# Order of a visit, z of early pairs, and where second-stage weights are decoded, in a fused linear-attention and feed-forward kernel

## The chip, the cores and the metric

The kernel runs on one core of a Trainium2 chip. The core has five instruction queues that run side by side and wait for each other through semaphores: TensorE (PE in the profile; PEld is its weight loading), VectorE (DVE), ScalarE (ACT), GpSimd (POOL) and SyncE (SP), which here only issues DMAs. PE writes its results to PSUM, from where DVE and ACT take them. The metric is the time of one execution on the device, in microseconds; lower is better.

## The reference

There are 8 batches of 8 heads, 576 tokens and head size 64. Then the heads are joined to 4608 tokens of 512 features, which go through a feed-forward network (FFN) of 2048 hidden features.

```python
def phi(x):
    proj = np.einsum('bhsd,df->bhsf', x, w_phi)            # 64 -> 128 features
    proj = proj - np.max(np.abs(proj), axis=-1, keepdims=True)
    return np.concatenate([np.exp(proj), np.exp(-proj)], axis=-1)
q_p, k_p = phi(q), phi(k)
kv  = np.einsum('bhsf,bhsd->bhfd', k_p, v)
z   = np.sum(k_p, axis=2)
num = np.einsum('bhsf,bhfd->bhsd', q_p, kv)
den = np.einsum('bhsf,bhf->bhs', q_p, z)[..., None] + 1e-06
x   = joined heads of num / den                            # 4608 x 512
h = x @ w_in                                               # 512 -> 2048
g = np.maximum(h, 0.0) + alpha * np.minimum(h, 0.0)
out = g @ w_out                                            # 2048 -> 512
```

The FFN's weights are double precision. The kernel gets them as pairs of 32-bit words, decodes them, and splits each into a high and a low part. Activations are split in the same way, so each FFN product is three matmuls: high by high, low by high, high by low (L494 to L496 and L500 to L502).

## The kernel before

**Attention by pairs.** Two heads make a pair; 32 pairs are numbered in the order in which they run (four pairs to a batch). The work on one pair is spread over several *visits*: in visit j, PE works on the projections of pairs j and j+1, on kv and z of pair j-1, and on the numerators and denominators of pair j-2. The names in the profile are:

- `raw`: k and q as loaded; `pj`, `pl`: their projections in PSUM (L297). DVE takes the largest magnitude of each row (`m`, L300) and subtracts it (`t`, L301).
- `xk`, `k` (in the program `k4`): exponentials of k, four full tiles of 128 tokens and one of 64, on ACT (L314, L309).
- `kv`: one PSUM tile with k's features by v (L338) and, in its third part, z (L355), by a product with ones. `y` and `z` on DVE (L323 to L331) add the k tiles before that product. For pairs below ZP = 9, called early here, only `y` is made, which adds tiles in twos, and PE adds up the rest; for the others DVE adds up all five tiles.
- `ks`, `kt`, `sf`: the copy of `kv` on ACT (L365), its transpose on PE (L370), and the copy of that (L374). `qt`, `qf`: the transposed t of q (L381, L384) and its exponentials (L392, L394).
- `n`: numerators (L403), two halves, copied by ACT to `s` (L414). `d`: denominators (L421), copied to `ds` (L431). A small DMA lays them out over partitions, DVE inverts them (L440, L441), a DMA writes them to HBM (`rec_d`), another spreads them over the rows (`rr`, L449), POOL multiplies (L454), and a DMA stores the tokens (`x_d`, L457).

`pl` of one head, `kt`, `qt`, the two halves of `n` and `d` all take turns in two PSUM buffers (`ps_m`). A projection takes turns in three others.

**The FFN in two stages.** Hidden blocks of 128 are numbered 0 to 15. The first stage (blocks 0 to 4) runs over nine chunks of 512 tokens while attention is still running: a visit holds some 30 FFN matmuls. Its partial results go to HBM (`part_d`). The second stage (blocks 5 to 15) goes over all chunks again, adds the partial results and stores. For each block, ACT takes two halves of the activation from PSUM (`r`, `g`, L228, L229), DVE joins them (`g`, L233), ACT casts the high part (`gh`, L119), DVE subtracts to get the low part (`gl`, L123). The tokens are split likewise, into `xh` (DVE, L120) and `xl` (POOL, L123).

**Decoding.** A weight block is decoded in four pieces of 256 columns: load (SP, L152), scale (ACT, L163), split (four DVE instructions, L171 to L174), add (POOL, L179), high (ACT, L119), low (POOL, L123), store. Blocks 0 to 4 come in the early visits, two pieces to a visit. Blocks 5 to 9 come from visit 12.5 on, 0.95 visits apart, and are stored to HBM (`w_d`); at the turn to the second stage, when attention's memory is free, they are loaded by DMAs that POOL issues. Blocks 10 to 12 are decoded in place from time 37.8 on. Blocks 13 to 15 are decoded after the first stage has closed, between the products of the second.

**What sets the order.** All the work up to that close is a list of small functions, each with a time in units of a visit. The list is sorted by time, and PE, SP, DVE and ACT execute in just that order; POOL's order is left to a scheduler. The function `places` (L57) holds the times of attention's steps after the pair's number: `ka` is kv, `kz` z, `p` the projections, `n` and `d` the numerators and denominators, `s` and `ds` their copies, `ko` the copy of kv, `ks` DVE's sums of k. `FG` (L93) holds the times of the join, the cast and `gl` after a block's last matmul; `WT` (L95) those of a decode's stages.

## Time and profile before

| | us |
|---|---|
| median of 3 runs (lowest to highest) | 1194.63 (1193.9 to 1195.11) |
| the profiled execution, in all | 1196.74 |
| its span from the first to the last instruction | 1195.0 |
| mean granted TensorE clock | 0.989 |
| chain that ended last: share of PE, of DVE | 53%, 4% |
| HBM traffic | 103 GB/s over the span |

An instruction of the profile is given by its engine, source line and operands, out<-in, with the buffers' numbers left out. A row of a wait says who waited for whom. A row of a timeline begins with the start in us from the beginning of the span and the duration; what stands in brackets is the idle time of that engine before it and what ended that. A PE matmul's end is modelled. Attention runs until about 560 us; the first stage's last chunks close at about 660 us; what follows is the second stage alone.

### The profile page before, as it was taken

How to read it: one execution, taken by the hardware profiler on the slowest of the kernel's cores; microseconds unless marked ns; L12 is line 12 of the kernel's file. 1: busy time of each engine (PE TensorE's matmuls, PEld its weight loads, DVE VectorE, ACT ScalarE, POOL GpSimd, SP SyncE). 2: the span in 40 equal slices, each digit the busy share in tenths (PEclk: the TensorE clock that was granted, in tenths of full speed). 3: DMA queues.
4: the chain of work that ended last, by engine and by line, in shares of the span. 5: the costliest groups of instructions: out<-in, count | busy, mean ns of one | idle time of the engine just before them, and what ended most of it. 6: DMA issues, size and time to landing. Idle time of an engine off the chain costs nothing.

```text
span 1195.0 us, 18168 instructions
## 1 busy us (share of the span) xinstructions
PE 1137.0 (95%) x7088; PEld 871.4 (73%) x7088; DVE 690.7 (58%) x1179; ACT 542.6 (45%) x1113; POOL 209.0 (17%) x210
## 2 busy tenths in 40 slices
PE   6887999999998999999999989999999999999998
PEld 5554667677676667766887768888888888888886
DVE  6988796887786888783366953333333333333322
ACT  2665554646465555655245533333333332333322
POOL 0234313131232323231243520000000000000000
PEclk9999899999999999999999999999999999999999
DMA  3456426453544445436332511111202020303020
GB/s 122 126 159 184 127 78 184 132 171 108 179 152 143 143 119 163 143 123 249 128 114 86 171 55 52 39 68 33 73 25 81 17 90 2 104 1 106 1 71 36
DMA packets 67910, 124.24 MB, mean 104 GB/s; under 512 B 14192, under 2 KB 19440, under 8 KB 67184
## 3 DMA queue, kind: packets, MB, share of 16 engines
q1 hardware_dynamic: 67104, 117.83, 31.0%
q0 software_dynamic: 720, 5.24, 1.2%
q8 instruction: 56, 0.92, 0.3%
q14 instruction: 30, 0.25, 0.1%
HBM read 89.20 MB, written 33.70 MB: 103 GB/s over the span
## 4 chain that ended last, share of the span: by engine, by line
PE 53%; DVE 4%; issue 1%; ACT 1%; DMA 0%; POOL 0%; ACTq 0%; DVEq 0%; SPq 0%
PE h L494 8%; PE h L495 8%; PE h L496 8%; PE po L502 7%; PE po L500 7%; PE po L501 7%; PE o L500 1%; PE o L501 1%; PE o L502 1%; DVE g L233 1%; PE kv L338 1%; PE d L421 1%; DVE ew L173 1%; PE n L403 0%; DVE aw L171 0%
## 5 line engine op out<-in xcount | busy, mean ns | idle before, releaser
L233 DVE SCALAR_TENSOR_TENSOR g<-r,aln,g 128x512 f32<-128x512 f32 x144 | 114.0, 792 | 305.5 <-ACT g L229 303.6
L228 ACT ACTIVATE r<-h 128x512 f32<-128x512 f32 x144 | 86.4, 600 | 288.3 <-PE h L496 288.2
L500 PE MATMUL po<-gh,w 128*128 128x512 f32 x396 | 155.0, 391 | 0.0
L501 PE MATMUL po<-gh,w 128*128 128x512 f32 x396 | 155.0, 391 | 0.0
L502 PE MATMUL po<-gl,w 128*128 128x512 f32 x396 | 154.4, 393 | 0.6 <-DVE gl L123 0.6
L123 DVE TENSOR_TENSOR gl<-g,gh 128x512 fp32r<-128x512 f32 x144 | 102.4, 711 | 83.0 <-ACT gh L119 82.9
L119 ACT CAST gh<-g 128x512 fp32r<-128x512 f32 x144 | 89.8, 624 | 93.5 <-DVE g L233 93.4
L300 DVE TENSOR_REDUCE m<-pj 128x4 f32<-128x512 f32 x128 | 87.1, 680 | 20.6 <-PE pj L297 20.6
L297 PE MATMUL pj<-w_sb,raw 64*128 64x128 f32 x1024 | 82.6, 298 | 14.1 <-DVE t L301 6.7
L179 POOL TENSOR_TENSOR aw<-ew,aw 128x256 f32<-128x256 f32 x64 | 58.3, 912 | 211.3 <-DVE ew L174 198.4
L297 PEld LDWEIGHTS pj<-w_sb,raw 64*128 64x128 f32 x1024 | 71.5, 204 | 31.0 <-issue 23.2
L301 DVE TENSOR_TENSOR t<-pj,m 128x512 f32<-128x512 f32 x128 | 88.5, 692 | 5.0
L494 PE MATMUL h<-x2hl,w 128*128 128x512 f32 x220 | 86.5, 393 | 4.4 <-ACT w L119 4.4
L502 PEld LDWEIGHTS po<-gl,w 128*128 128x128 f32 x396 | 74.3, 188 | 18.2 <-DVE gl L123 1.9
L495 PE MATMUL h<-x2hl,w 128*128 128x512 f32 x220 | 86.5, 393 | 0.3 <-POOL w L123 0.3
L496 PE MATMUL h<-x2hl,w 128*128 128x512 f32 x220 | 86.4, 393 | 0.0
L501 PEld LDWEIGHTS po<-gh,w 128*128 128x128 f32 x396 | 74.3, 188 | 16.6
L500 PEld LDWEIGHTS po<-gh,w 128*128 128x128 f32 x396 | 74.3, 188 | 16.5
L229 ACT ACTIVATE g<-h 128x512 f32<-128x512 f32 x144 | 85.9, 597 | 0.0
L500 PE MATMUL o<-gh,w 128*128 128x512 f32 x180 | 76.4, 424 | 0.4 <-ACT os L545 0.3
L494 PE MATMUL h<-xh,w 128*128 128x512 f32 x180 | 75.9, 422 | 0.0
L403 PE MATMUL n<-qf,sf 128*64 128x288 f32 x512 | 70.5, 416 | 3.1 <-DVE t L301 3.1
(84 smaller groups left out, 2131.5 us busy)
## 6 DMA issues: line engine op xcount, KB each, us to landing
xr<-x_d SPq DMA_DIRECT2D x18, 1024.0 KB
raw<-kq_dram SPq DMA_DIRECT2D x31, 576.0 KB
v<-v_dram SPq DMA_DIRECT2D x32, 320.0 KB
rr<-rec_d SPq DMA_DIRECT2D x64, 144.0 KB
x_d<-s SPq DMA_DIRECT2D x32, 288.0 KB
part_d<-os SPq DMA_DIRECT2D x36, 256.0 KB
pt<-part_d SPq DMA_DIRECT2D x9, 1024.0 KB
raww<-w_in_dram SPq DMA_DIRECT2D x32, 256.0 KB
```

The lines of the kernel that those rows point to most:

```text
L119: return act.copy(dst, src)
L123: return eng.tensor_tensor(dst, src, f(hi), op=ALU.subtract)
L233: dve.scalar_tensor_tensor(g, st["r"], aln[:, ff : ff + 1], g, op0=ALU.mult, op1=ALU.add)
L297: pe.matmul(dst[h, j], lhsT=c["raw"][hs, ts], rhs=w_sb[hs], start=True, stop=True)
L300: dve.tensor_reduce(m, src, axis=AX.X, op=ALU.max, apply_absolute_value=True)
L301: dve.tensor_tensor(t[:, h, j : j + w], src, m.unsqueeze(2).broadcast_to([P, w, FD]), op=ALU.subtract)
L494: pe.matmul(ps, lhsT=wt[0][:, ws], rhs=xh, start=n == 0, stop=False)
L495: pe.matmul(ps, lhsT=wt[1][:, ws], rhs=xh, start=False, stop=False)
L496: pe.matmul(ps, lhsT=wt[0][:, ws], rhs=xl, start=False, stop=n == NK - 1)
L500: pe.matmul(ps, lhsT=wt[2][:, ws], rhs=gh, start=first, stop=False)
L501: pe.matmul(ps, lhsT=wt[3][:, ws], rhs=gh, start=False, stop=False)
L502: pe.matmul(ps, lhsT=wt[2][:, ws], rhs=gl, start=False, stop=last)
```

## The change

The steps of a visit get other times, so z and the denominators come first, then kv, then the numerators; the next pair's k projection comes last, or, for early pairs, just before the numerators. Early pairs make no `y`: z is added up by PE from the five k tiles. All second-stage blocks are decoded by the sorted list: 5 to 9, then 13 to 15, which are now stored to HBM as well, then 10 to 12 in place. Pieces follow each other at 0.70 visits. The raw tile has a third buffer and takes the place of the output tile of stored pieces. The late blocks 13 to 15 are loaded by three 1 MB DMAs on POOL's queue once the first stage has closed, and the second stage's loop has no decoding in it. The join, cast and `gl` have later times, `GL` with the last chunks; the loads of alpha and `w_phi` move from SP's queue to ACT's; the small projection takes its PSUM buffer before the large ones.

```diff
 NA = 5
+NL = NF2 - 8
...
-W2Z = 31.5
+W2D = 0.70
...
-        p=(-0.997 if early else -0.993, 0.0),
+        p=(-0.9955 if early else -0.993, 0.0),
         ke=(-0.26, 0.0011),
-        ks=(0.0035 if early else 0.0015, 0.0022, 0.0026),
-        ka=1.001,
-        kz=1.0055,
-        ko=1.0075,
+        ks=(0.0015, 0.0022, 0.0026),
+        kz=1.0002,
+        ka=1.0012,
+        ko=1.0025,
...
-        n=2.004,
-        d=2.0060,
-        s=2.0050,
-        ds=2.0076,
+        d=2.0004,
+        ds=2.0008,
+        n=2.005,
+        s=2.0055,
...
-FG = (0.15, 0.32, 0.45)
+FG = (0.15, 0.34, 0.52)
+GL = (0.20, 0.42, 0.58)
+TL = 31.4
+WL = dict(load=-0.75, scale=-0.40, split=0.0, add=0.28, high=0.60, low=0.80, store=0.95)
-WT = dict(load=-0.90, scale=-0.25, split=0.0, add=0.15, high=0.42, low=0.55, store=0.90)
+WT = dict(load=-0.70, scale=-0.25, split=0.0, add=0.15, high=0.42, low=0.55, store=0.90)
...
-    nc.sync.dma_start(al, alpha)
+    act.dma_start(al, alpha)
...
-        raw = wdec[0].tile([P, n, 2], U32, tag="wraw", name=f"raw{tag}", bufs=W_BUFS_[0])
+        raw = w1t.tile([P, n, 2], U32, tag="wraw", name=f"raw{tag}", bufs=W_BUFS + 1)
...
-            wo = w1t.tile([P, 2, n], F32R, tag="wo", name=f"ow{ff}_{z}_{o}", bufs=1)
+            wo = raw.rearrange("p a b -> p (a b)").rearrange("p (t n) -> p t n", t=2).bitcast(F32R)
...
-    nc.sync.dma_start(w_sb, w_phi)
+    act.dma_start(w_sb, w_phi)
...
-            ps = [ps_pj.tile([P, 4, FD], F32, tag="pj", name=f"pj{i}_{ch}_{h}") for h in range(2)]
-            dst = {(h, j): ps[h][:, j] for h in range(2) for j in range(4)}
-            out, js = [], [0, 1, 2, 3]
+            dst, out, js = {}, [], [0, 1, 2, 3]
             if ch:
...
-                    out = [(h, 4, 1, p1)] + out
+                    out.append((h, 4, 1, p1))
+            ps = [ps_pj.tile([P, 4, FD], F32, tag="pj", name=f"pj{i}_{ch}_{h}") for h in range(2)]
+            dst.update({(h, j): ps[h][:, j] for h in range(2) for j in range(4)})
...
         def k_sum(step):
-            if i < ZP and step:
+            if i < ZP:
                 return
...
             if i < ZP:
-                y = c["y"].rearrange("p (a h) (n f) -> p a h n f", a=2, n=2)
-                zs = [y[:, :, :, j, :] for j in range(2)] + [c["x", 1][:, :, :, 0, :]]
+                zs = [c["x", 0][:, :, :, j, :] for j in range(4)] + [c["x", 1][:, :, :, 0, :]]
...
-    blocks = [(ff, z, o) for ff in range(NF1, NF1 + NA) for z in range(2) for o in range(0, 512, WN)]
+    late = (*range(NF1, NF1 + NA), *range(NF - NL, NF), *range(NF1 + NA, NF - NL))
+    blocks = [(ff, z, o) for ff in late for z in range(2) for o in range(0, 512, WN)]
...
-        todo += decode_at(W2A + (W2Z - W2A) * n / len(blocks), blk)
+        todo += decode_at(W2A + W2D * n, blk)
...
-    for n, blk in enumerate(
-        (NF1 + ff, z, o) for ff in range(NA, NA + ND) for z in range(2) for o in range(0, 512, WN)
-    ):
-        todo += decode_at(T2 + 2.4 + 0.7 * n, blk)
...
     for ff in range(NA + ND, NF2):
-        W[NF1 + ff] = weight_tile(w2b, f"w{NF1 + ff}")[0]
-    wdec[0] = ctx.enter_context(tc.tile_pool(name="w3t", bufs=1, side="right"))
-    W_BUFS_[0] = 4
-    late = decode_units(range(NA + ND, NF2))
-    for u in late[:LEAD]:
-        u()
-    late = late[LEAD:]
+        W[NF1 + ff], w2l[ff] = weight_tile(w2b, f"w{NF1 + ff}")
+    for ff in range(NA + ND, NF2):
+        pool.dma_start(w2l[ff], w_d[slot_d(NF1 + ff)])
     load_x(1)
-    for n in range(NB, NF2):
-        pass2(n, n + 1, LAG)
-        for u in late[:2]:
-            u()
-        late = late[2:]
+    pass2(NB, NF2, LAG)
     pass2(NF2, len(seq), 0)
```

The order on three places of the engines follows, with the tiles' own numbers: the digits after a name are the pair (`kv17`, `d16`) or chunk and block (`gl1_2_3`: stage 1, chunk 2, block 3); the last number only tells buffers apart. First PE, at the start of a late visit. Before:

```order
L338 MATMUL kv17_3399<-xk17_3141,v17_3078 64x256 x8
L338 MATMUL kv17_3399<-k4_1_123,v17_3078 64x256 x2
L403 MATMUL n16_0_3417<-qf16_3296,sf16_3274 64x288 x4
L403 MATMUL n16_1_3422<-qf16_3296,sf16_3274 64x288 x4
L355 MATMUL kv17_3399<-z17_3206,ones_119 32x128 x4
L421 MATMUL d16_3434<-qf16_3296,sf16_3274 32x288 x8
L297 MATMUL pj19_0_0_3444<-w_sb_117,raw19_3265 128x128
```

Now:

```order
L353 MATMUL kv17_3468<-z17_3292,ones_119 32x128 x4
L419 MATMUL d16_3473<-qf16_3365,sf16_3348 32x288 x8
L336 MATMUL kv17_3468<-xk17_3213,v17_3149 64x256 x8
L336 MATMUL kv17_3468<-k4_1_123,v17_3149 64x256 x2
L401 MATMUL n16_0_3506<-qf16_3365,sf16_3348 64x288 x4
L401 MATMUL n16_1_3511<-qf16_3365,sf16_3348 64x288 x4
L296 MATMUL pj19_0_0_3520<-w_sb_117,raw19_3336 128x128
```

z and the denominators moved from behind the numerators to the front; the projection stays last, and behind it come three FFN matmuls and the transpose `kt`.

Second DVE, at the border to that same visit, where the third `gl` of a chunk stands. Before:

```order
L233 SCALAR_TENSOR_TENSOR g1_2_3_3328<-r1_2_3_3327,aln_74,g1_2_3_3328 128x512
L440 TENSOR_SCALAR d9_15_3289<-d9_15_3289 128x9
L441 RECIPROCAL r9_15_3348<-d9_15_3289 128x9
L123 TENSOR_TENSOR gl1_2_3_3367<-g1_2_3_3328,gh1_2_3_3356 128x512
L300 TENSOR_REDUCE m18_1_14_3384<-pl18_1_3373 128x1
L301 TENSOR_TENSOR t18_1_3369<-pl18_1_3373,m18_1_14_3384 128x128
```

Now, after the eight subtractions and their maxima and the sums of pair 18:

```order
L329 TENSOR_TENSOR z18_3501<-z18_3501,k4_0_121 128x512
L299 TENSOR_REDUCE m19_0_00_3530<-pj19_0_0_3520 128x4
L300 TENSOR_TENSOR t19_0_3519<-pj19_0_0_3520,m19_0_00_3530 128x512
L299 TENSOR_REDUCE m19_0_10_3533<-pj19_0_1_3521 128x4
L300 TENSOR_TENSOR t19_0_3519<-pj19_0_1_3521,m19_0_10_3533 128x512
L126 TENSOR_TENSOR gl1_2_3_3540<-g1_2_3_3401,gh1_2_3_3431 128x512
```

`gl1_2_3` moved from ahead of pair 18's subtractions to behind those of pair 19's first projection.

Third SP's queue in an early visit. Before:

```order
L444 DMA rec_d_58<-r9_4_1200 128x9
L510 DMA xr1_0_1266<-x_d_57 128x4x512
L275 DMA raw9_1273<-kq_dram 128x1152
L152 DMA raww2_1_0_1275<-w_out_dram 128x512
L449 DMA rr4_1280<-rec_d_58 64x576 x2
L279 DMA v8_1286<-v_dram 128x640
L435 DMA d9_5_1288<-ds5_1264 128x1x9
L152 DMA raww2_1_256_1319<-w_out_dram 128x512
L457 DMA x_d_57<-s4_1073 128x576
```

Now:

```order
L442 DMA rec_d_58<-r9_4_1265 128x9
L508 DMA xr1_0_1306<-x_d_57 128x4x512
L274 DMA raw9_1313<-kq_dram 128x1152
L447 DMA rr4_1318<-rec_d_58 64x576 x2
L278 DMA v8_1324<-v_dram 128x640
L433 DMA d9_5_1326<-ds5_1251 128x1x9
L157 DMA raww2_1_0_1333<-w_out_dram 128x512
L157 DMA raww2_1_256_1367<-w_out_dram 128x512
L455 DMA x_d_57<-s4_1132 128x576
```

The first raw-weight load moved from ahead of `rr` to behind the denominators' DMA.

## The prediction

> **What bounds the kernel now.** I read the busy totals first, then the stretches of the program, then who waits for whom, then single visits.

> ```profile
> PE 1137.0 (95%) x7088; PEld 871.4 (73%) x7088; DVE 690.7 (58%) x1179; ACT 542.6 (45%) x1113; POOL 209.0 (17%) x210
> ```

> TensorE (PE) is busy 1137.0 of 1195.0 us, so at most 58 us of idle time, and what a lowered clock costs, can be won. The table by stretches says where they lie. Its columns are length, then busy time and instruction count of PE, of its weight loads, VectorE (DVE), ScalarE (ACT) and GpSimd (POOL), then granted clock, DMA share, GB/s.

> ```profile
> 28.96:148.82 119.86, 99.77 (x1032) 66.70 (x1030) 99.41 (x197) 73.10 (x166) 41.06 (x46) 0.94 0.50 149
> 148.82:540.35 391.53, 375.51 (x3055) 270.31 (x3053) 311.55 (x542) 219.78 (x480) 103.02 (x91) 0.99 0.45 141
> 540.35:630.00 89.65, 88.45 (x446) 69.55 (x446) 41.02 (x66) 40.52 (x82) 27.30 (x26) 1.00 0.47 161
> 630.00:720.00 90.00, 84.36 (x354) 66.37 (x353) 63.34 (x114) 43.35 (x93) 35.83 (x38) 0.98 0.35 117
> 720.00:1195.00 475.00, 469.81 (x2045) 383.33 (x2043) 157.35 (x230) 157.20 (x280) 0.00 (x0) 1.00 0.14 48
> ```

> PE idles 20.1 us in the early visits (119.86 - 99.77; pairs below 9, where the first weights are decoded), 16.0 us in the late visits, 1.2 and 5.6 us around the turn to the second stage, and hardly after it. The last stretch has no decode and no attention, and the change leaves it alone. Next, PE's own waits (total, times, longest):

> ```profile
> PE d L421 <- ACT s L414: 28.9, 18, 4.6
> PE pj L297 <- DVE t L301: 6.7, 8, 1.2
> PE pj L297 <- DMA raw<-kq_dram: 4.9, 1, 4.9
> ```

> Half of the idle time is one wait: the denominators `d` need a PSUM buffer that the numerators `n` just filled, and ACT must copy `n` out (`s`) first. Two late visits show what a visit costs with and without it, and one of the long waits in detail:

> ```profile
> 293.99:315.21 21.22, 18.47 (x141) 13.18 (x139) 13.60 (x27) 12.62 (x26) 3.79 (x4) 0.92 0.48 148
> 315.21:331.72 16.51, 16.51 (x142) 12.09 (x140) 15.52 (x24) 7.99 (x18) 6.90 (x6) 1.00 0.51 171
> ```

> ```profile
> 293.00 1.06 PE L297 MATMUL pj<-w_sb,raw 64*128 64x128 f32 x16
> 296.16 0.69 DVE L123 TENSOR_TENSOR gl<-g,gh 128x512 fp32r<-128x512 f32 x1 [2.58 <-ACT gh L119]
> 298.64 0.43 PE L355 MATMUL kv<-z,ones 128*32 128x128 f32 x8
> 300.58 0.72 ACT L309 ACTIVATE k<-t 64x256 f32<-64x256 f32 x2 [3.14 <-DVE t L301]
> 301.21 0.67 ACT L414 COPY s<-n 128x288 f32<-128x288 f32 x2
> 301.63 1.36 PE L421 MATMUL d<-qf,sf 128*32 128x288 f32 x16 [2.56 <-ACT s L414]
> 302.93 2.08 PE L297 MATMUL pj<-w_sb,raw 64*128 64x128 f32 x16
> ```

> ```profile
> 302.00:304.00 2.00, 2.00 (x26) 1.24 (x20) 1.17 (x2) 0.65 (x2) 0.00 (x0) 0.62 0.06 17
> ```

> The last row is the table by stretches again, for 2 us. The undisturbed visit is PE throughout: 16.51 busy of 16.51, so 16.5 us is its floor. The disturbed one takes 4.7 us more: DVE sits 2.58 us at `gl` for ACT's cast, ACT's `k` exponentials wait for the DVE work behind `gl`, `s` stands behind `k`, PE waits 2.56 us for `s`, and then the clock falls (0.62 just after), so `pj` takes 2.08 where it took 1.06 at the visit's start.

> In the early visits the same wait has another start:

> ```profile
> 61.63 0.33 SPq L457 DMA_DIRECT2D x_d<-s  x1
> 63.15 0.64 PE L355 MATMUL kv<-y,ones 128*32 128x128 f32 x16
> 63.61 0.40 PE L355 MATMUL kv<-k,ones 128*32 128x128 f32 x8
> 65.31 0.70 ACT L414 COPY s<-n 128x288 f32<-128x288 f32 x2 [3.38 <-DMA x_d<-s]
> 65.76 1.18 PE L421 MATMUL d<-qf,sf 128*32 128x288 f32 x16 [1.75 <-ACT s L414]
> 67.19 0.33 SPq L152 DMA_DIRECT2D raww<-w_in_dram  x1
> 67.61 1.12 SPq L449 DMA_DIRECT2D rr<-rec_d  x2
> ```

> and in the list of waits, for SP's queue:

> ```profile
> SPq L152 <- DVE ew L174: 110.8, 29, 9.9
> ```

> ACT waits 3.38 us for the store that frees an `s` buffer. That store hangs on `rr`, and `rr` stands in SP's queue behind a raw-weight load that waits for DVE's decode: 29 such blocks, 110.8 us in all.

> **The change, part by part,** against the profiled span of 1195.0 us.

> *Order of a visit.* The denominators now come before the numerators, with kv between. The same matmuls run, so PE's floor stays; `d` no longer needs a buffer of `n`. The wait for `s` cannot vanish altogether: the next to need a PSUM buffer of `n` is the transpose `kt`. How much cover has it? In a late visit `n` starts 1.4 us later than before (0.43 of z and about 1.1 of `d`, ahead of it now, less an overlap); behind it stand the next projections (1.1 us) and three FFN matmuls (0.7 us at 30 us for 132, quoted below) before `kt`, where only z's 0.43 stood before `d`. Together ACT has some 2.8 us more, above the 2.56 of the wait shown. In addition the third `gl` of a chunk moves behind the next visit's subtractions, so the 2.58 us of DVE standing still goes too. I take the late idle time, 16.0 + 1.2, down to 1.2: **-16**; kept at both ends: -9 (half stays) and -17.

> *Early visits.* Here `kt` follows `n` directly, so ACT gains only the shift of z and `d`, 1.1 + 1.1 us, and loses z's 1.0 of cover: +1.2 us against waits such as 1.75. Three other things help. A third raw buffer and later loads take the decode's wait out from ahead of `rr` in SP's order. The 9 `y` additions leave DVE. And a decode block stands behind the subtractions that PE waits for, where two stood ahead of them.

> ```profile
> L323 DVE TENSOR_TENSOR y<-xk 128x1024 f32<-128x1024 f32 x32 | 41.0, 1281 | 1.7 <-PE kv L355 1.7
> L171 DVE TENSOR_SCALAR aw<-aw 128x256 uint32<-128x256 uint32 x64 | 30.1, 471 | 16.0 <-ACT aw L163 16.0
> L172 DVE SCALAR_TENSOR_TENSOR aw<-raww,aw 128x256 uint32<-128x256 uint32 x64 | 37.9, 595 | 1.8
> L173 DVE TENSOR_SCALAR ew<-aw 128x256 uint32<-128x256 uint32 x64 | 23.5, 369 | 1.8
> L174 DVE SCALAR_TENSOR_TENSOR ew<-raww,ew 128x256 f32<-128x256 uint32 x64 | 29.9, 468 | 1.8
> ```

> DVE loses 9 x 1.28 = 11.5 us there, leaving 88 of its 99.4. DVE was busy 83% of this stretch; in 105 us it would be 84%, so it allows that length. Of 20.1 us idle I leave 5: **-15**, between -6 (only `y` and half the `d` waits count) and -17.

> *z of early pairs from five tiles.* It reads the four k tiles instead of the two halves of `y`: 16 more instructions per pair. By 0.64 us for the 16 of `y`, or by the 0.43 us that separate 24 instructions (63.15 to 64.01) from 8: 9 x 0.43 = **+4**, at most 5.8. Nothing hides this; it is PE time.

> *Clock.* 0.94 of 119.86 and 0.99 of 391.53 us are some 7 and 4 us lost. The lows follow waits of 2.5 us and more, most of which go: **-6**, between -2 and -9. [...]

> *All decoding in the first stage.* The last 12 of 44 blocks were decoded after the FFN's first pass had ended:

> ```profile
> 660.00:690.00 30.00, 25.96 (x110) 19.84 (x108) 29.96 (x55) 17.03 (x38) 20.20 (x20) 1.00 0.43 142
> 690.00:720.00 30.00, 28.71 (x117) 22.82 (x118) 14.96 (x24) 11.61 (x24) 5.10 (x7) 0.94 0.28 94
> 720.00:750.00 30.00, 30.00 (x132) 24.43 (x131) 10.45 (x16) 10.54 (x19) 0.00 (x0) 1.00 0.03 12
> ```

> ```profile
> w<-w_d POOLq DMA_DIRECT2D x5, 1024.0 KB, 10.3
> ```

> DVE is full there (29.96 of 30) and PE runs 110 and 117 matmuls where 132 fit: 37 x 0.227 = 8.4 us lost. These blocks now come earlier, and three 1 MB loads on POOL's queue bring the result back: **-8**, between -4 and -8.4. The five loads like them (last row) landed in 10.3 us each by the median; the cover is the five weight blocks that PE works through first, 5 x 24 x 0.227 = 27 us.

> The 12 blocks, and a spacing of 0.70 visits in place of 0.95, add 12 x 1.90 = 23 us to DVE in the late visits: 311.6 becomes 334 of some 375, plus about 0.03 us before each instruction (1.8 us for 64 in the rows of L172 to L174), 351 in all or 94%. The visit at 315.21 ran at its floor with 15.52 + 0.7 of 16.51 on DVE, so a fully loaded DVE need not stop PE. But the third `gl` is now ready at about the moment when PE asks for it (both some 10 us into the visit, by the rows' durations). At the turn the casts and `gl` stand up to 0.13 visits later than before, with DVE less than half busy there (41.0 of 89.65 us) to make it up. On SP's queue come 12 more stores, each held until POOL has made the low half. A raw load now also waits until the block three before it is stored. Behind both stand `rec_d`, `rr` and `x_d`; but `x_d` is issued half a visit, some 8 us, before ACT needs its `s` buffer, which is the cover. For new waits of these kinds I set **+2**, between 0 and +16 (a third of the late visits losing what the disturbed one lost above its wait, 2.1 us).

> *Start.* SP issues the first raw k tile ahead of alpha and `w_phi`, which move to ACT's queue; PE waits 4.9 us there. Two issues of some 0.4 us go from ahead of it, but `w_phi` is no sooner: **-0.5**, between 0 and -0.9.

> Sum: -16 - 15 + 4 - 6 - 8 + 2 - 0.5 = -39.5, so 1155.5 us by the span. The profiled run took 1196.74 in all, and the median of the three runs, 1194.63, is 0.4 below the span: **1155 us**.

> **The rivals.**

> *The wait only moves.* `kt` stands where `d` stood, and ACT is just as late, since `s` still waits for the store of an older pair and for `k`. For it: 3.38 us on the store, and the short cover in early visits. Against it: SP's order. Half of the two idle terms and of the clock term stay: 1195 - 8 - 7.5 - 3 + 4 - 8 - 0.5 = 1172.

> *The late weights come too late.* If the three loads run one after the other, they take 3 x 10.3 = 31 us against 27 of cover: a stop of 4 us and some 2 of low clock, 1161. Against it: PE needs the first of them, not the third, at the end of the cover.

> *DVE becomes the bound, and it gets slower.* In the late visits DVE has 311.6 busy, 542 x 0.03 = 16 between instructions, and so 64 us of waits of its own, mostly for ACT's `r`, `g` and `gh`. If these stay while 23 + 2 us of decode come in, the visits stretch. All 64 kept give 311.6 + 16 + 25 + 64 = 417, or +25 on 391.5. Every POOL addition can add to that:

> ```profile
> 126.41 1.50 DVE L171 TENSOR_SCALAR aw<-aw 128x256 uint32<-128x256 uint32 x1
> 126.17 1.59 POOL L454 TENSOR_TENSOR s<-s,rr 128x576 f32<-128x576 f32 x1
> ```

> ```profile
> L179 POOL TENSOR_TENSOR aw<-ew,aw 128x256 f32<-128x256 f32 x64 | 58.3, 912 | 211.3 <-DVE ew L174 198.4
> L123 POOL TENSOR_TENSOR ow<-aw,ow 128x256 fp32r<-128x256 f32 x20 | 15.7, 787 | 55.3 <-ACT ow L119 55.3
> ```

> A 0.47 us instruction took 1.50 beside a POOL multiplication. If every POOL instruction of the 12 blocks stops DVE for its length, 12 x 1.7 = 20 us more: +45, and 1195 + 45 - 15 - 3 + 4 - 8 - 0.5 = 1217. It decides, as slower, once the late visits grow by more than 22 us. [...] Against this rival: the visit at 315.21, where POOL had 6.90 us of work and PE did not stop.

> **How the numbers follow.** Forecast 0.62; the wait only moves 0.19; weights too late 0.05; DVE the bound 0.10, two thirds of it slower than before, the rest near it; better than all terms' middle, below 1145, 0.04. The best ends (-17, -17, +4, -9, -8.4, 0, -0.9) give 1147, and the extra DVE slack in early visits some us less: low 1143. Upward the range must hold the moved wait (1172) with the small ends of the other terms, about 11 more: high 1183. Above it is the DVE rival. About 0.2% (2.4 us) is what runs of this kernel can tell from no change: faster 0.90, same 0.03, slower 0.07.

> **What would show it.** Right: `d` waiting for `s` gone from PE's waits, `kt` for `ks` or `s` below 5 us in all; late visits at 16.5 to 17 us; early ones near 11.5; 130 or more matmuls in every 30 us after the turn; clock at 1.00 in nearly all slices. Wrong: `kt` or `o` with a dozen waits of 1 us or more, DVE near 100% in the late visits, or a PE stop before the last three weight blocks.

## The result, and the profile after

| | before | after |
|---|---|---|
| median (lowest to highest), us | 1194.27 (1192.62 to 1195.11) | 1164.13 (1163.43 to 1168.59) |
| ratio of the times, 95% interval | | 0.9757, [0.9731, 0.9784] |
| span of the profiled execution, us | 1195.0 | 1166.8 |
| mean granted clock in it | 0.989 | 0.994 |

The kernel is 30 us faster; some 39 were forecast. The profiled execution of after was the longest of its four, 1168.59 us, so its rows add up to some 4 us more than the median.

The totals of after, as its page has them:

```profile
PE 1132.6 (97%) x7232; PEld 871.9 (75%) x7232; DVE 687.1 (59%) x1170; ACT 543.0 (47%) x1113; POOL 216.8 (19%) x213
```

Now the table by stretches (columns as in the prediction). The first three rows are cut at the same events as there: the kv products of pairs 1 and 9, of pair 9 and the last pair, and the end. Then come five early visits (1 to 5), two late ones (25 and 29), and pieces at and behind the turn. A visit is counted here from the kv product of the pair with its number to that of the next pair.

```profile
31.71:130.11 98.40, 92.66 (x1130) 64.60 (x1127) 85.44 (x182) 68.47 (x159) 41.44 (x44) 1.00 0.57 170
130.11:513.33 383.22, 375.41 (x3057) 270.51 (x3053) 334.45 (x576) 227.58 (x497) 121.60 (x106) 0.99 0.49 155
513.33:1166.80 653.47, 642.84 (x2821) 519.24 (x2817) 247.23 (x372) 233.82 (x435) 49.83 (x52) 0.99 0.22 76
31.71:85.78 54.07, 53.97 (x709) 37.31 (x705) 48.31 (x110) 40.02 (x95) 18.07 (x22) 1.00 0.59 170
405.86:426.53 20.67, 18.41 (x144) 13.20 (x140) 15.53 (x31) 11.93 (x26) 4.71 (x6) 0.92 0.63 192
477.44:499.20 21.76, 18.43 (x143) 13.21 (x139) 17.05 (x33) 12.35 (x27) 4.85 (x4) 0.92 0.54 172
560.00:570.00 10.00, 4.51 (x12) 3.12 (x11) 6.18 (x10) 5.06 (x11) 3.52 (x4) 0.73 0.25 91
600.00:630.00 30.00, 29.87 (x131) 24.08 (x130) 17.60 (x27) 12.82 (x27) 12.00 (x12) 1.00 0.21 69
630.00:660.00 30.00, 30.00 (x133) 24.74 (x133) 10.29 (x15) 12.86 (x24) 1.63 (x3) 1.00 0.53 193
690.00:720.00 30.00, 30.00 (x131) 24.41 (x131) 9.55 (x14) 11.34 (x21) 0.00 (x0) 1.00 0.14 53
```

The ledger against before, with the repeated execution of after (experiment 1) beside it:

| stretch, us | before | after | difference | after again |
|---|---|---|---|---|
| start to kv of pair 1 | 28.96 | 31.71 | +2.8 | 32.51 |
| early visits | 119.86 | 98.40 | -21.5 | 97.77 |
| late visits | 391.53 | 383.22 | -8.3 | 380.35 |
| kv of the last pair to the end | 654.65 | 653.47 | -1.2 | 653.67 |

The first and the last difference are mostly a matter of where the cut lies: kv now stands behind z and d, about 2 us later in its visit. PE's first wait grew only from 4.94 to 5.14 us, and from the first `h` of the second stage to the end the two spans have 615.2 and 614.9 us. So nothing was won at the start or in the second stage, more than forecast was won in the early visits, and about half of what was forecast in the late ones.

PE's own waits of after (total, times, longest):

```profile
PE o L500 <- DVE gl L126: 6.8, 5, 3.3
PE pj L296 <- DVE t L300: 5.6, 7, 1.2
PE pj L296 <- DMA w_sb<-w_phi_dram: 5.1, 1, 5.1
PE po L498 <- issue: 3.4, 1, 3.4
...
PE po L500 <- DVE gl L126: 2.1, 1, 2.1
...
PE kt L368 <- ACT s L412: 0.4, 1, 0.4
```

The wait of `d` for `s`, 28.9 us before, is gone, and `kt` did not inherit it: 0.4 us. New are waits for `gl`, and a stop of 3.4 and 2.1 us at the turn. Both can be followed in the timeline. First the turn:

```profile
552.45 0.41 SPq L202 DMA_DIRECT2D w_d<-raww  x1
...
553.96 0.37 SPq L508 DMA_DIRECT2D xr<-x_d  x1
...
555.03 1.65 SPq L157 DMA_DIRECT2D raww<-w_out_dram  x2
...
561.62 0.43 ACT L166 ACTIVATE aw<-raww 128x256 f32<-128x256 f32 x1 [5.70 <-DMA raww<-w_out_dram]
...
562.90 0.62 ACT L122 CAST gh<-g 128x512 fp32r<-128x512 f32 x1
...
563.62 0.47 PE L498 MATMUL po<-gh,w 128*128 128x512 f32 x1 [3.39 <-issue]
...
566.42 0.80 PE L500 MATMUL po<-gl,w 128*128 128x512 f32 x1 [2.09 <-DVE gl L126]
```

ACT stands 5.70 us at the scale of a raw weight piece. That load was issued at 555.03, behind a store at 552.45 and the 1 MB load of `xr`. In order behind the scale are `r`, `g` and the cast `gh`, which ends at 563.52; PE goes on 0.10 us later. The page calls PE's wait "issue", that is, it names no releaser; that `gh` released it is read from where it ends. The clock over these 10 us is 0.73.

Then visit 25, where the third `gl` of an FFN chunk is late:

```profile
411.57 1.42 POOL L452 TENSOR_TENSOR s<-s,rr 128x576 f32<-128x576 f32 x1 [5.11 <-DMA rr<-rec_d]
411.65 1.89 DVE L329 TENSOR_TENSOR z<-z,k 128x512 f32<-128x512 f32 x1
...
416.10 0.68 DVE L126 TENSOR_TENSOR gl<-g,gh 128x512 fp32r<-128x512 f32 x1
...
416.84 0.51 PE L500 MATMUL o<-gl,w 128*128 128x512 f32 x1 [2.27 <-DVE gl L126]
```

The sum `z` took 1.89 us, and its like takes 0.69 us elsewhere. It began while POOL's multiplication `s<-s,rr` ran. `gl` comes behind four more instructions of DVE, and PE waits for `gl`.

### The profile page after: what moved, and what is told of

Read it like the earlier page. It is cut to its first block, busy times and chain, and to the rows that moved or that the text cites. A ratio compares the mean times of both kernels' runs of the same rounds, so it can differ in the third digit from the quotient of the medians.

```text
span 1166.8 us, 18415 instructions
## 1 busy us (share of the span) xinstructions
PE 1132.6 (97%) x7232; PEld 871.9 (75%) x7232; DVE 687.1 (59%) x1170; ACT 543.0 (47%) x1113; POOL 216.8 (19%) x213
## 3 DMA queue, kind: packets, MB, share of 16 engines
q0 software_dynamic: 1152, 8.39, 1.9%
## 4 chain that ended last, share of the span: by engine, by line
PE 80%; DVE 10%; DMA 5%; ACT 3%; issue 2%; POOL 1%; SPq 0%; ACTq 0%; DVEq 0%
PE h L492 10%; PE h L493 10%; PE h L494 10%; PE po L500 8%; PE po L498 8%; PE po L499 8%; PE kv L336 4%; PE pj L296 4%; PE n L401 4%; PE o L500 3%; PE o L498 3%; PE o L499 2%; DVE m L299 2%; DVE t L300 2%; PE qt L382 2%
## 5 line engine op out<-in xcount | busy, mean ns | idle before, releaser
L232 DVE SCALAR_TENSOR_TENSOR g<-r,aln,g 128x512 f32<-128x512 f32 x144 | 111.4, 774 | 316.2 <-ACT g L228 316.1
L498 PEld LDWEIGHTS po<-gh,w 128*128 128x128 f32 x396 | 74.9, 189 | 20.5 <-issue 3.8
L296 PE MATMUL pj<-w_sb,raw 64*128 64x128 f32 x1024 | 77.4, 289 | 10.8 <-DVE t L300 5.6
L499 PEld LDWEIGHTS po<-gh,w 128*128 128x128 f32 x396 | 74.9, 189 | 16.7
L296 PEld LDWEIGHTS pj<-w_sb,raw 64*128 64x128 f32 x1024 | 67.2, 196 | 25.2 <-issue 21.5
L500 PE MATMUL o<-gl,w 128*128 128x512 f32 x180 | 72.8, 404 | 7.1 <-DVE gl L126 6.8
## 6 DMA issues: line engine op xcount, KB each, us to landing
xr<-x_d SPq DMA_DIRECT2D x18, 1024.0 KB
pt<-part_d SPq DMA_DIRECT2D x9, 1024.0 KB
```

The costliest lines, as they stand in the source:

```text
L232: dve.scalar_tensor_tensor(g, st["r"], aln[:, ff : ff + 1], g, op0=ALU.mult, op1=ALU.add)
L296: pe.matmul(dst[h, j], lhsT=c["raw"][hs, ts], rhs=w_sb[hs], start=True, stop=True)
L498: pe.matmul(ps, lhsT=wt[2][:, ws], rhs=gh, start=first, stop=False)
L499: pe.matmul(ps, lhsT=wt[3][:, ws], rhs=gh, start=False, stop=False)
L500: pe.matmul(ps, lhsT=wt[2][:, ws], rhs=gl, start=False, stop=last)
```

## The experiments

All times are medians; ratios are against the kernel before, run on the same chip.

**1. The changed kernel again** (no edit).

> The changed kernel once more, for its own spread. If the two long waits of `o` for `gl` in late visits (2.3 and 3.3 us, visits 25 and 29) and the stop at the turn (`o` for `gl` 2.1 us behind `po` 3.4 us) belong to its order, they return within 0.5 us each, at 1164 us. If they were an accident of the profiled execution, which was 4 us above the median, at least one of the two late ones is under 1 us here.

1163.32 us, 0.9744 [0.9717, 0.9772]. The waits returned: 2.04 us in visit 25, 2.80 in visit 29, 3.37 and 1.61 at the turn. So they belong to the order of the changed kernel and not to one execution.

**2. The order alone,** on the kernel before.

```diff
-        kz=1.0055, ka=1.001, ko=1.0075
-        n=2.004, s=2.0050, d=2.0060, ds=2.0076
+        kz=1.0002, ka=1.0012, ko=1.0025
+        d=2.0004, ds=2.0008, n=2.005, s=2.0055
```

(With it `p` and `ks` of the early pairs as in the change, and kv's tile taken with its product.)

> The kernel before with the new times of a visit alone: `z` and `d`, `kv`, `n` and `s`, then the next k tiles; `y`, the decode's place and its buffers as before. Theory (the order takes the `d` wait of 28.9 us away and what it does to the clock): late visits from 391.5 to 372 - 376 us, early ones from 119.9 to 108 - 114 us, 1168 to 1178 us. Rival (without the freed VectorE and SP's order ACT is as late as before, and `kt` or `n` waits in its place): 1185 to 1194 us.

1176.63 us, 0.9867 [0.9829, 0.9905]: some 16 of the 30 us. Its early and late stretches, SP's wait for the decode, ACT's wait for the store before and here, and one of three late stops:

```profile
32.05:137.51 105.46, 94.43 (x1018) 63.66 (x1014) 95.81 (x190) 68.60 (x160) 44.94 (x44) 0.98 0.55 163
137.51:522.36 384.85, 374.72 (x3057) 270.51 (x3053) 310.63 (x539) 221.04 (x480) 103.61 (x91) 0.99 0.46 145
```

```profile
SPq L152 <- DVE ew L174: 94.8, 32, 5.8
```

Before, then here:

```profile
ACT s L414 <- DMA x_d<-s: 14.9, 5, 3.4
```

```profile
ACT s L414 <- DMA x_d<-s: 0.7, 1, 0.7
```

```profile
278.21 0.69 DVE L123 TENSOR_TENSOR gl<-g,gh 128x512 fp32r<-128x512 f32 x1 [2.59 <-ACT gh L119]
...
282.63 0.73 ACT L309 ACTIVATE k<-t 64x256 f32<-64x256 f32 x2 [2.86 <-DVE t L301]
...
289.39 0.62 ACT L119 CAST gh<-g 128x512 fp32r<-128x512 f32 x1 [4.26 <-DVE g L233]
...
290.41 0.90 PE L384 MATMUL qt<-ident,t 128*128 128x128 f32 x3 [2.35 <-ACT qf L392]
```

The early stretch fell by 14.4 us, more than the 6 to 12 of the theory. ACT hardly waits for the store any more, although there are two raw buffers as before and SP still stands at the raw loads. The late stretch fell by 6.7 instead of 15 to 20. With the third `gl` in its old place DVE still stands 2.59 us for ACT's cast, ahead of the next pair's subtractions. DVE's join `g` comes late in turn, `gh` waits 4.26 us for it, and `qf` stands behind `gh`: PE waits 2.35 us (in three visits 2.35, 3.42 and 2.16). Taking the wait off `d` was not enough; by this trace `gl` had to move as well, which was not run with the order alone.

**3. The old order with all the rest of the change.**

```diff
-        d=2.0004, ds=2.0008, n=2.005, s=2.0055     # and kz, ka, ko, p
+        n=2.004, s=2.0050, d=2.0060, ds=2.0076     # and kz, ka, ko, p as before
```

> The changed kernel with the old times of a visit: numerators `n`, then `s`, `d`, `ds`, and `kv` and `z` after them; z from five tiles, the decode in the first stage and the `gl` times stay as changed. Theory (the order is what frees the late visits): `d` waits for `s` again, some 25 us in 10 to 18 waits, visits of 18 to 21 us among the late ones, the early visits at 12 to 14 us; 1180 to 1192 us by the median. Rival (the third raw buffer, the later loads and the freed VectorE did most of it, and the order little): `d` waits under 8 us in all, early visits under 11.5 us, 1162 to 1172 us.

1191.99 us, 0.9985 [0.9963, 1.0007]: without the order the rest of the change is worth nothing that can be told.

```profile
29.83:140.53 110.70, 99.05 (x1160) 68.17 (x1158) 89.56 (x186) 72.93 (x166) 40.61 (x46) 0.98 0.52 156
140.53:535.94 395.41, 378.47 (x3055) 270.76 (x3053) 330.45 (x576) 225.96 (x496) 118.83 (x106) 0.99 0.48 150
```

```profile
PE d L419 <- ACT s L412: 18.5, 13, 3.8
```

In the profiled execution the early visits are 9.2 us shorter than before. The late visits take 395.4 us, 3.9 more than before, since they now carry more decoding; the new order brings them to 380.4 (experiment 1), 15 us less. The `d` waits of 18.5 us were below the 25 named.

**4. `y` made on DVE again for early pairs,** z from its halves.

```diff
-            if i < ZP:
+            if i < ZP and step:
...
-                zs = [c["x", 0][:, :, :, j, :] for j in range(4)] + [c["x", 1][:, :, :, 0, :]]
+                zs = [y[:, :, :, j, :] for j in range(2)] + [c["x", 1][:, :, :, 0, :]]
```

> The changed kernel with the 9 early pairs' `y` made on VectorE again and z read from its two halves: 144 matmuls less on TensorE, 9 times 1.28 us more on VectorE. Theory of the prediction (z of five costs 4 us of TensorE time and VectorE would be nearly full with `y`): early visits at 11.2 to 11.8 us and not the 10.81 us that they take now, bound by VectorE, 1166 to 1172 us. Rival (the early visits' stops were the order's and SP's queue's alone, and `y` has room): early visits at 10.81 - 0.45 = 10.35 us, 1158 to 1161 us.

1168.46 us, 0.9794 [0.9765, 0.9823]. Four of its early visits, 2 to 5:

```profile
41.75:87.74 45.99, 43.51 (x504) 29.17 (x501) 44.19 (x94) 33.64 (x78) 16.25 (x17) 1.00 0.56 164
```

They take 11.50 us each in place of 10.81, with DVE busy 96%; 2.1 of PE's 2.5 us of idle time there end with DVE's `t`, so DVE bounds them. Visit 1, still without a gap on PE, takes 10.38: 0.43 below 10.81, which is the price named for z from five tiles. It is paid on every early pair, and it buys a PE that no longer waits: the early stretch is 104.04 us here and 97.77 in experiment 1.

**5. Raw loads ahead of `rr` in SP's queue again.**

```diff
-WT = dict(load=-0.70, ...
+WT = dict(load=-0.90, ...
```

> The changed kernel with the raw loads of the decode 0.2 visits earlier again, so that they stand ahead of `rr` in SP's queue as before. Theory (a raw load that waits for its buffer held `rr`, the stores and so ACT's `s`): SP's queue waits at the raw loads again, with three buffers some 30 to 60 us in all, and ACT's `s` waits for `x_d`; early visits at 11.2 to 12 us, 1167 to 1173 us. Rival (the third buffer alone takes the wait out, or the new order has room for a late `s`): early visits stay at 10.81 us, 1162 to 1165 us.

1167.76 us, 0.979 [0.976, 0.9821]; its interval overlaps that of experiment 1. The early stretch is the same, 97.80 us:

```profile
32.89:130.69 97.80, 92.86 (x1130) 64.59 (x1126) 87.36 (x182) 68.60 (x159) 41.47 (x44) 1.00 0.57 171
```

The edit did not bring back the wait that it was to bring back. In the early stretch SP stands at a raw load for the decode once, 1.8 us (29.7 in experiment 2, 55.0 before); over the whole run it is 21.1 us in six waits, about as in after (20.4), where 30 to 60 were named. So with three raw buffers the place of the loads costs nothing in the early visits. What the third buffer is worth by itself was not run. The median lies in the theory's range all the same, but the early visits have no part in that: by the spans the run is 3.1 us longer than experiment 1, 0.4 at the start, 0.9 in the late visits and 1.8 behind them, where the turn's waits are 4.3, 1.6 and 1.4 us in place of 3.4, 1.6 and 0.6.

**6. The third `gl` earlier,** ahead of the sums `y` and `z`.

```diff
-FG = (0.15, 0.34, 0.52)
+FG = (0.15, 0.34, 0.471)
```

> The third `gl` of each FFN chunk of the first stage stands 0.05 visits earlier on VectorE: behind the next pair's subtractions on `p1`, but ahead of its `y` and `z` sums. Theory (a late `gl` is what the new order costs in the late visits): no wait of `o` for `gl` above 1 us there, visits 25 and 29 at 16.5 to 17.2 instead of 20.7 and 21.8 us, 8 us less from kv of pair 9 to kv of pair 31, and 1156 to 1160 us by the median. Rival A (the old place of `gl` was what made the exponentials late, so moving back brings that back): `qt`, `kt` or `d` waits of 1 us and more for ACT, other visits at 18 to 21 us, 1162 to 1170 us. Rival B (the waits are of the one profiled run): under 1 us of difference, 1163 to 1165 us.

1162.75 us, 0.9739 [0.9707, 0.9771]: no change that can be told. In visit 25 the wait for `gl` is gone and PE waits 0.89 us for `qf` instead; the visit takes 17.6 us, in experiment 1 19.1. Visit 29 kept its 2.80 us: the chunk there takes its times from `GL`, which the edit left alone and the expectation had overlooked.

**7. The pieces at the turn later.**

```diff
+        at = WT if t < TL else WL if t < 36.5 else {**WL, "load": -1.10}
...
-        todo += decode_at(W2A + W2D * n, blk)
+        todo += decode_at(W2A + W2D * n + (0.6 if n >= 34 else 0.0), blk)
```

> The decode pieces from the 35th on stand 0.6 visits later, and the raw loads of those in the FFN-only part 0.35 visits earlier against their scale on ACT. Theory (the stop at the turn is a raw load that lands late and holds ACT at the scale of `aw`, 5.7 us, so that `h2` has no PSUM buffer and `gl` is late): no PE wait above 0.5 us between the last attention visit and 600 us, clock 1.00 there, 8 to 9 us less from kv of pair 31 to the end, 1154 to 1157 us by the median. Rival (the stop comes from the 1 MB load of `xr`, which keeps the DMA engines busy, and from `r` and `g` behind ACT's other work): a stop of 3 us or more stays, 1161 to 1165 us.

1156.56 us, 0.969 [0.9664, 0.9716]: 6.8 us less than experiment 1 on the same chip. The last stretch and the turn:

```profile
508.48:1157.70 649.22, 640.33 (x2821) 517.56 (x2817) 247.60 (x375) 234.36 (x435) 49.23 (x52) 1.00 0.22 77
560.00:570.00 10.00, 8.55 (x38) 6.69 (x38) 9.19 (x12) 0.75 (x2) 8.06 (x9) 1.00 0.11 28
```

The stop of 3.4 us and the low clock are gone, and the last stretch is 4.5 us shorter than in experiment 1, where 8 to 9 were named. Of the spans' difference of 6.6 us another 2.4 lie in the late visits, whose order here is the same. The expectation said no wait above 0.5 us, and that missed: waits for `gl` of 1.19, 1.45 and 1.14 us remain up to 600 us. ACT also still waits for raw loads (10.1 us in all, 13.4 in after), but not where `r`, `g` and `gh` of the next product stand behind it. Which of the two edits did it was not separated.

**8. Both, and `w_phi` ahead of alpha on ACT's queue.**

```diff
+    w_sb = cst.tile([P, FD], F32, name="w_sb")
+    act.dma_start(w_sb, w_phi)      # now ahead of act.dma_start(al, alpha)
```

> Both edits, the earlier `gl` and the later pieces at the turn, and the load of `w_phi` ahead of alpha's on ACT's queue. If both losses are what the trace of the changed kernel shows and they do not depend on each other: 8 + 8 us less, and up to 0.5 us at the start, 1147 to 1151 us by the median. If one only moves the other's wait: 1154 to 1160 us. If neither is a cause: 1163 to 1165 us.

1155.79 us, 0.9682 [0.9654, 0.971], and 1155.64 us, 0.9684, when it ran again beside the next two:

> The kernel with the earlier third `gl`, the later pieces at the turn and `w_phi` first, once more, to stand beside the two below: 1155 to 1157 us by the median, with the wait of `o` for `gl` of 2.8 us in visit 29 (19.6 or, with a lowered clock, 21.2 us long) as in every run so far, since the FFN chunk of that visit takes its three places from the other table, of 0.58 for the third `gl`, which the earlier edit did not touch.

The turn's gain is there, `gl`'s is not, as experiment 6 had shown. PE's first wait is 4.0 us in place of 5.1: with `w_phi` first the start does get shorter.

**9. The last chunk's third `gl` earlier too.**

```diff
-ffn1_units(b, FG if t1 < TL else GL)
+ffn1_units(b, FG if t1 < TL else (0.20, 0.42, 0.471))
```

> The same with the third `gl` of the last FFN chunk beside attention at 0.471 too. Theory (the `y` and `z` sums and the subtractions on `p0` ahead of `gl` on VectorE are what makes it late): visit 29 at 16.5 to 17.5 us with no wait for `gl` above 0.5 us, 2 to 4 us less in all than its like without, 1152 to 1154 us by the median. Rival (the wait goes over to `qt` for ACT's `qf`, as it did in visit 25, with 0.9 and 1.6 us): visit 29 at 17.5 to 19 us, 1154 to 1156 us.

1153.1 us, 0.9667 [0.9642, 0.9691]. Visit 29 has no wait any more:

```profile
472.80:489.38 16.58, 16.58 (x143) 12.01 (x139) 15.25 (x28) 9.69 (x22) 4.78 (x4) 1.00 0.52 170
```

In the run of experiment 8 beside it this visit took 20.5 us. The 2.5 us between the medians are within what the intervals overlap; the visit itself shows the effect.

**10. ACT's scale later in the FFN-only part.**

```diff
-        at = WT if t < TL else WL if t < 36.5 else {**WL, "load": -1.10}
+        at = WT if t < TL else WL if t < 35.5 else {**WL, "load": -1.10, "scale": -0.12}
```

> The same as the kernel with the last chunk's `gl` earlier, and in the FFN-only part ACT's scale of a raw block stands 0.28 visits later, next to VectorE's first instruction on it, so that a late raw load holds ACT less. Theory (what is left of the `gl` waits between 525 and 615 us, some 5 us in e6, comes from ACT standing at that scale for the load, 2.2 and 4.3 us): these waits under 2 us in all, 2 to 4 us less, 1149 to 1152 us. Rival (they come from the decode pieces ahead of `gl` on VectorE, and a later scale makes those wait at VectorE instead): no gain or 1 to 3 us more.

1156.07 us, 0.9694 [0.9673, 0.9714], so no gain, as the rival said. (The edit also takes in the pieces between 35.5 and 36.5, whose loads move as well; the two were not separated.) The other waits of the turn are about as in experiment 9, and a new one of 2.25 us, with a fall of the clock, stands at 608 us, where DVE's pieces stand ahead of `gl`:

```profile
608.28 0.50 PE L501 MATMUL o<-gl,w 128*128 128x512 f32 x1 [2.25 <-DVE gl L126]
```

**11. POOL's multiplication `s<-s,rr` earlier in the late visits** (the expectation below calls it an addition). Across the runs from the changed kernel on, visit 25 had a wait of anything from 0.4 to 2.3 us, with the same instructions. In experiment 7 its sums were not stretched, and `gl` came in time but for 0.59 us:

```profile
411.73 0.69 DVE L330 TENSOR_TENSOR z<-z,k 128x512 f32<-128x512 f32 x1
...
412.63 1.43 POOL L453 TENSOR_TENSOR s<-s,rr 128x576 f32<-128x576 f32 x1 [6.09 <-DMA rr<-rec_d]
...
415.73 0.50 PE L501 MATMUL o<-gl,w 128*128 128x512 f32 x1 [0.59 <-DVE gl L126]
```

The multiplication starts when `rr` lands. Here that is after the last sum has ended; in after it was just before that sum. So the last kernel moves the multiplication:

```diff
-        dv=2.80, rd=2.82, rr=3.001, x=3.20, xs=3.45    # late pairs
+        dv=2.66, rd=2.68, rr=2.90, x=3.02, xs=3.30
```

> The kernel with the last chunk's `gl` earlier too (e8), and in the late visits the reciprocal, its store and load `rr`, GpSimd's addition `s<-s,rr` and the store `x_d` all some 0.15 visits earlier, so that the addition lies beside the subtractions on `p1`, which read PSUM, and not beside the sums `y` and `z`. In the late visits of e8 14 of the 22 had a sum that began while that addition ran and took 1.0 to 1.2 us longer than its 1.22 or 0.69 us. Theory (that is what makes `gl` and so `qf` late in the one run by 2.0 and in the other by 0.4 us, in visit 25 with the same instructions): at most 3 of the 22 visits have such a sum, the waits of `qt` for `qf` fall from 3.0 to under 1 us, visit 25 takes 16.7 to 17.2 us, and the median is 1149 to 1152 us. Rival A (the subtractions or the decode are held in the sums' place): as many instructions are held, and the time stays at 1152 to 1155 us. Rival B (the wait in visit 25 has another cause): the sums are free of it and the wait of 0.4 to 2.0 us stays.

1152.37 us, 0.9658 [0.964, 0.9676]: no difference from experiment 9 that can be told, and in the range of rival A. 8 visits still have a sum that was held for about 1 us, where at most 3 were named, and visit 25 is one of them:

```profile
406.95 1.56 POOL L453 TENSOR_TENSOR s<-s,rr 128x576 f32<-128x576 f32 x1 [3.18 <-DMA rr<-rec_d]
...
407.15 2.43 DVE L323 TENSOR_TENSOR y<-xk 128x1024 f32<-128x1024 f32 x1
...
415.54 0.66 PE L383 MATMUL qt<-ident,t 128*128 128x128 f32 x4 [1.69 <-ACT qf L391]
```

The multiplication did not get clear of the sums. What the runs have instead is a set of like visits. With `gl` in the changed kernel's place, visit 25 with a held sum waited 2.27, 2.04, 2.16 and 1.50 us, and without one 0.59 (after and experiments 1, 5, 4 and 7). With `gl` ahead of the sums it waited 1.63, 2.04, 2.00 and 1.69 held, 0.89 and 0.41 not held. By these a held sum costs PE about 0.7 to 1.7 us in that visit. This is a comparison of eleven executions, not a kernel in which the multiplication was out of the way.

## Why the prediction was right or wrong

The time lies inside the range, 9 us above the forecast; the direction and the main mechanism were right. By the terms of the sum:

| term | forecast | measured |
|---|---|---|
| late visits' idle time of PE | -16 | -8.2 (16.0 to 7.8), in the repeat -9.1 |
| early visits' idle time | -15 | -14.4 (20.1 to 5.7) |
| z from five tiles | +4 | +0.43 a pair, 3.9 on nine |
| clock | -6 | -5 (12.0 lost before, 6.8 now) |
| decode out of the second stage | -8 | -0.3 from its first `h` to the end |
| start | -0.5 | +0.2 |

The measured column adds up to -24, and the profiled spans differ by 28. The forecast's "new waits" have no row: what they cost is inside the rows of the late visits, of the clock and of the decode. Their own size is given below, and is not to be added a second time.

**Order of a visit: right.** `d` for `s` went, `kt` for `s` is 0.4 us. Experiments 2 and 3 put the order's worth at 16 us without the rest and 29 us with it, and the rest's at nothing that can be told without the order.

**Late visits: the step that failed is "new waits +2".** It named the place (the third `gl` is ready at about the moment when PE asks for it) and priced it too low. Visits 25 and 29 took 20.7 and 21.8 us where the other late visits with as much FFN work took 16.5 to 17.5: 8 to 9 us in the profiled run and about 7 in the repeat, lowered clock included. With the turn, where waits of 5.5 us and a clock of 0.73 over 10 us were added, the term measured some 17 us, in the repeat as well, a little above its upper bound of 16. I had said that in a disturbed visit both gains, `d`'s and `gl`'s, would be kept; experiments 1, 2 and 6 show a balance: `gl` ahead of the subtractions makes the exponentials late, `gl` behind the sums is itself late, and between them, `qf` is. Only the last chunk had a place free of all three (experiment 9).

**Early visits: idle time right, the rest better.** Visits 1 to 5 run at 10.81 us, below the 11.5 I looked for; nearly all of the 5.7 us of idle time that is left lies in visits 7 and 8. PE's busy time in the stretch fell by 7.1 us, though it has 98 more matmuls, for z, some 2.6 us at 0.43 for 16. The clock, 0.94 of 119.86 us before and 1.00 now, accounts for 6.8 us; some 3 us are not attributed. The order, with the new places of the early pairs' projections and sums, shortened the stretch by 14.4 us (experiment 2). Taking `y` off DVE, with its PE price paid, gave 6.3 more (experiment 4). The reading that the store chain behind `rr` had to be freed by SP's order does not hold: with the new order alone ACT's wait for the store fell from 14.9 to 0.7 us, while SP still stood at the raw loads. With three buffers the place of the loads made no difference (experiment 5); the third buffer and the place of the decode blocks were not run by themselves.

**Clock: size right by luck.** Before, 12.0 us were lost to a lowered clock: 6.8 in the early visits, 3.4 in the late ones, 1.7 behind the turn. They came behind waits of 2.1 to 4.6 us, two of them (2.13 and 2.19 us) below the 2.5 named; for the small end of the term, -2, no run shows a reason. None of these falls is left, where I let about half of them stay. But the new waits brought falls of their own, in visits 25 and 29 and at the turn, which cost 6.8 us.

**z: size right.** I charged 4 us and called it unhidden, and it is. With `y` off DVE, which stands in the term of the early visits, the pair of edits is a gain of 6.3 us.

**Decode out of the second stage: right mechanism, spent at the turn.** Behind the turn the stretches of 30 us shown hold 131 to 133 matmuls, as said. The part of the sum that failed is the cover at the turn: I counted on "DVE less than half busy there" and did not ask how far ahead of its use a raw load is issued there. In the FFN-only part a unit of time is three blocks' 36 `h` matmuls at 0.227 us, 8.2 us, so the lead of 0.35 units between a raw load and its scale is 2.9 us, and here the load landed 6.5 us after its issue, behind that of `xr`. That `xr` is what delayed it is read from their order alone. Experiment 7 gets 4.5 us of the last stretch back. Waits for `gl` of 1.2, 1.5 and 1.1 us between 525 and 600 us remain in it, where DVE now decodes; the rest of the 8 us was not traced.

**Start: wrong by 0.7 us.** `w_phi` was moved to another queue but behind alpha there. Ahead of alpha PE's first wait is 4.0 us in place of 5.1 (experiment 8), 4.6 in experiment 11.

**The rivals.** "The wait only moves": refuted for the whole, since `kt` waits 0.4 us; in visits 25 and 29 a part of it did move, to `o` and `qt`. "Late weights too late": refuted, PE has no wait behind the three loads issued from 633.71 us. "DVE the bound": its first part is refuted, since late visits with DVE busy 16.0 of 16.5 us ran without a gap. Its second part, POOL holding DVE, is at work in 14 of 22 late visits of after, for 0.9 to 1.25 us each, and is hidden in all but visits 25 and 29.

The best version tried is that of experiments 9 and 11, 1152 to 1153 us, 0.966 to 0.967 of the time before.

## What to carry to other kernels

When a PSUM wait is taken away by reordering, follow the in-order engine that was late to the next instruction which somebody waits for; here ACT and DVE were freed at `s` and became late at `gl` (2.3 and 3.3 us in visits 25 and 29). If work is moved into a stage that is paced in units of that stage's own time, work out its leads in microseconds again: a lead of 0.35 units would be 5.8 us in a late visit and was 2.9 us at the turn. An added cost on the bound engine can be a gain if it unloads the engine that makes it wait (here 0.43 us of PE a pair, and visits 2 to 5 at 10.81 us in place of 11.50): price both in the same visit.

## What the runs showed of the hardware that was not expected

**Beside POOL some DVE instructions took longer and others did not.** Counted are instructions that began with at least 0.2 us of a POOL instruction to go. In the late visits of experiment 9, 15 sums `y` or `z` began so beside POOL's `s<-s,rr`, and all took longer: 14 by about 1.08 us on average, some 0.14 us less than was left of the multiplication, and the last, with 0.30 us to go, by 0.16. All 11 small `d<-d` were longer too (in the late visits of after they took 0.69 to 1.26 us so, and 0.16 with POOL idle). The 18 `m<-pj` and `t<-pj,m`, which read PSUM, and the 13 reciprocals `r<-d` took their usual time (0.68, 0.69 and 0.22 us). An instruction already running was not disturbed: 12 sums within which a POOL instruction began took their usual 1.22 or 0.69 us, and there it was POOL's that took longer, `s<-s,rr` up to 2.43 us where 1.42 is usual. (The first sum below took its 0.69 us, though the multiplication began within it; the next took 1.73, and the reduction from PSUM behind it, begun beside POOL's next instruction, its usual 0.68.) From visit 25 of experiment 9:

```profile
406.98 0.69 DVE L327 TENSOR_TENSOR z<-y 128x512 f32<-128x512 f32 x1
...
407.12 1.83 POOL L453 TENSOR_TENSOR s<-s,rr 128x576 f32<-128x576 f32 x1 [5.15 <-DMA rr<-rec_d]
...
407.77 1.73 DVE L330 TENSOR_TENSOR z<-z,k 128x512 f32<-128x512 f32 x1
...
409.31 0.80 POOL L126 TENSOR_TENSOR raww<-aw,raww 128x256 fp32r<-128x256 f32 x1 [0.35 <-ACT raww L122]
...
409.43 0.68 DVE L300 TENSOR_REDUCE m<-pj 128x4 f32<-128x512 f32 x1
```

**A fall of the clock cost 1.71 us, and came behind waits of 1.88 to 3.42 us, but not behind all of them.** Taking the waits of PE in all the runs that had no other within 8 us: 63 of 0.7 to 1.72 us, and none was followed by a fall; 30 of 1.88 to 3.42 us, and 21 were, each with the clock at half for 3.41 us, so 1.71 us lost. The one of 3.42 us was not. The same visit with and without it, from experiment 9 and from experiment 8's second run, PE having waited 2.00 and 2.04 us:

```profile
401.78:422.13 20.35, 18.35 (x144) 13.19 (x140) 15.01 (x29) 11.39 (x26) 5.07 (x6) 0.92 0.61 195
```

```profile
402.60:421.35 18.75, 16.71 (x143) 12.01 (x139) 15.04 (x29) 11.33 (x26) 4.43 (x5) 1.00 0.63 197
```
